# A recurrence beside a feed-forward block: loads of a later step moved behind a step's output matmuls, and a sigmoid moved into the step's outputs

## The chip, the cores and the metric

The kernel runs on one core of one Trainium2 chip. The time is the device time of one execution in microseconds (us). The core's engines work side by side, each through its own list of instructions in order: TensorE (PE in the profile; its weight loads are PEld), VectorE (DVE), ScalarE (ACT), GpSimd (POOL) and SyncE (SP), which here only issues DMA transfers. An instruction that must wait for another engine holds up all that stands behind it on its own engine; this holds for the transfers on SP's queue as well.

## The reference

Three stages follow one another. The first is a recurrence with a matrix state (an mLSTM) over 4 batches, 8 heads, 768 tokens, 40 numbers per head:

```python
for t in range(S):
    m_new = np.maximum(f_gate[:, :, t] + m, i_gate[:, :, t])
    f_stab = np.exp(f_gate[:, :, t] + m - m_new)
    i_stab = np.exp(i_gate[:, :, t] - m_new)
    C = f_stab * C + i_stab * np.einsum('bhd,bhe->bhde', vt, kt)
    n = f_stab * n + i_stab * kt
    y[:, :, t] = sigmoid(o_gate[:, :, t]) * (C @ q) / np.maximum(np.abs(n @ q), 1.0)
```

Its output, 3072 tokens of 320 numbers, goes through a gated block, `(sigmoid(x @ w_gate) * (x @ w_val)) @ w_out` with 1536 hidden numbers, and that through a second, `(h * relu6(h + 3) / 6) @ w_out` with 2048.

## The kernel before, in words

**The recurrence by steps.** The 768 tokens are cut into 6 chunks of 128. Within a chunk the recurrence is written as matrix products; between chunks the state `cst` goes on. One step is one chunk and one batch, named (c,b); there are 24. A step needs three loaded tiles: `qk` (queries and keys, L209), `vko` (values, keys by token, output gate, L212) and `dec`, the rows of decay factors, broadcast to all partitions (L220). Each of the three has two slots, so the tile of step b+2 lies where that of step b was, and its load waits until the last reader of step b is done: for `qk` the output matmuls (L442), for `dec` the matmuls of L453, for `vko` the gated output `yo` (L502), which VectorE makes.

**A step has three pieces.** `att0`: the scores (L360), the values with the input gate (`vi`, L351), two scans that make the decays (L386), two weightings of the scores with them (L401), and in the kernel before also the output gate's sigmoid (L407). `att1`: the matmuls of the outputs (L442, L453) and of the state (L468), the denominators (L485 to L494), `y` and `yo` (L351, L502), the state update (L523). `att2`: a transposition on TensorE (L534), split into a rounded and a remaining part (ScalarE L539, VectorE L540). The scores' PSUM banks are emptied by the weightings, and there are two such banks, which the scores, the outputs and the transposition share. So a transposition must wait for a weighting.

**The feed-forward block runs beside it.** `m1_h` makes 128 hidden numbers for 512 tokens: eight matmuls into one PSUM bank (L552 to L559), eight into another; ScalarE makes the sigmoid (`g`, L578), VectorE the product (L579), which empties the second bank, and both split it (`gh` L565, `gl` L566). `m1_out` multiplies with the output weights (L594, L604), one or two such steps later. The pool `mm` of PSUM has three banks; two are `m1_h`'s, and the state matmuls take one as well. Between two steps of the block, at most one or two pieces of the recurrence are put in, by a list of numbers (`quota`).

**The weights of the second block are prepared meanwhile.** Raw weights are fetched (`raw`, L92), made to float (L116, L119) and stored (`w_dram`, L619). From the fourth chunk on every second step of the block calls `combine_w2`: it loads one transfer into `wa` (L651) and four small ones into its second half (L656), makes sums and differences on VectorE (L663), splits them (ScalarE `ws` L667, VectorE L668 and L673) and stores them (`ws_dram`, L677). The last part, L668 and L673, is called the ws block below.

**What sets the order.** The program is traced in Python in the order of these calls, and a scheduler then places each instruction on its engine's list. In the main loop, the loads of the step after the next are traced behind piece 2 (L881 to L883):

```python
if cp > 0 and piece == 2 and nxt[0] < NC:
    att_load(*nxt)
    dec_load(*nxt)
```

Of the kernel before, what the change touches and what calls it, by code (L numbers as in the profile page):

```python
# [20 lines left out]
NC = S // L  # L21
# [11 lines left out]
def mlstm_then_two_gated_ffn(  # L33
# [159 lines left out]
    def slot_f32(n, p=P):  # L193

        return wpool.tile([P, 1280], F32, tag="w", name="early", bufs=18)[:p, :n]

    def att_tiles(c, b):
        if c == 0 and b > 1:
            t = slot_f32(2 * NP * L).rearrange("p (a n l) -> p a n l", a=2, l=L)
            v = slot_f32(3 * DM).rearrange("p (a n) -> p a n", a=3)  # L200
            d = slot_f32(H * L).rearrange("p (h l) -> p h l", l=L)
        else:
            t = ap.tile([P, 2, NP, L], F32, tag="qk", name="qk")
            v = ap.tile([P, 3, DM], F32, tag="vko", name="vko")
            d = ap.tile([P, H, L], F32, tag="dec", name="dec")
        at[c, b] = {"qk": t, "vko": v, "dec": d}

    def qk_load(c, b):
        nc.sync.dma_start(out=at[c, b]["qk"], in_=qkT[c, b])  # L209

    def vko_load(c, b):
        nc.sync.dma_start(out=at[c, b]["vko"], in_=vko[c, b])  # L212

    def att_load(c, b):
        att_tiles(c, b)
        qk_load(c, b)
        vko_load(c, b)

    def dec_load(c, b):
        nc.sync.dma_start(  # L220
            out=at[c, b]["dec"].rearrange("p h l -> p (h l)"),
            in_=fz_dram[c, b * H : (b + 1) * H, :]
            .rearrange("h l -> (h l)")
            .rearrange("(o n) -> o n", o=1)
            .to_broadcast([P, H * L]),
        )
# [28 lines left out]
    last_exp = []  # L255
# [98 lines left out]
    def scores(c, b, ps):  # L354
        a = at[c, b]
        qk = a["qk"]
        a["s"] = [ps(), ps()]
        for h in range(H):
            p0 = 64 * (h % 2)
            nc.tensor.matmul(  # L360
                out=a["s"][h % 2][:, (h // 2) * L : (h // 2 + 1) * L],
                lhsT=qk[p0 : p0 + D, 1, h // 2, :],
                rhs=qk[p0 : p0 + D, 0, h // 2, :],
                start=h < 2,
                stop=h >= H - 2,
                skip_group_check=True,
            )
# [37 lines left out]
    def out_gate(c, b):  # L405
        o = at[c, b]["vko"][:, 2, :]
        nc.scalar.activation(out=o, in_=o, func=AF.Sigmoid)  # L407

    def att0(c, b, ps):
        scores(c, b, ps)  # L410
        if c == 1:
            values(c, b, True)
        value_ones(c, b)
        for n in range(2):
            decays(c, b, n)
        if c != 1:
            values(c, b, False)
        if c < NC - 1:
            values_end(c, b, c == 0)
        for n in range(2):  # L420
            weigh(c, b, n)

        with tc.issue_after(last_exp[-1]):
            out_gate(c, b)

    def att1(c, b, ps):

        outputs(c, b, ps)
        y = denominators(c, b)
        gated(c, b, y, c == 1 and b < 2)  # L430
        state(c, b)

    def outputs(c, b, ps):
        a = at[c, b]
        dec, vi = a["dec"], a["vi"]

        halves = [slice(t, t + 32) for t in range(0, L, 32)]
        if c > 0:
            o_ps = a["o_ps"] = ps()
            for n in range(NP):  # L440
                for tt in halves:
                    nc.tensor.matmul(  # L442
                        out=o_ps[tt, n * 2 * D1 : (n + 1) * 2 * D1],
                        lhsT=a["qk"][:, 0, n, tt],
                        rhs=cst[:, b, n, :],
                        start=n == 0,
                        stop=n == NP - 1,
                        skip_group_check=True,
                    )
        i_ps = a["i_ps"] = ps()  # L450
        for h in range(H):
            for tt in halves:
                nc.tensor.matmul(  # L453
                    out=i_ps[tt, h * D1 : (h + 1) * D1],
                    lhsT=dec[:, h, tt],
                    rhs=vi[:, h, :],
                    start=h == 0,
                    stop=h == H - 1,
                    skip_group_check=True,
                )  # L460
        if c < NC - 1:
            k_on = a["vko"].rearrange("p a n -> p (a n)")[:, DM:]
            c_ps = c_banks[c, b] = ps() if ps is any_ps else ps_mm()
            for h in range(H):
                p0 = 64 * (h % 2)

                for d in (0, 32):
                    nc.tensor.matmul(  # L468
                        out=c_ps[p0 + d : p0 + d + 32, (h // 2) * D1 : (h // 2 + 1) * D1],
                        lhsT=k_on[:, h * D + d : h * D + d + 32],  # L470
                        rhs=a["vd"][:, h, :],
                        start=h < 2,
                        stop=h >= H - 2,
                        skip_group_check=True,
                    )

    def denominators(c, b):
        a = at[c, b]
        i_v = a["i_ps"][:, : H * D1].rearrange("p (h d) -> p h d", d=D1)
        y = i_v  # L480
        den = a["den"] = ap.tile([P, H, 1], F32, tag="den", name="den")
        if c > 0:
            y = ap.tile([P, H, D1], F32, tag="y", name="y")
            o_v = a["o_ps"][:, : H * D1].rearrange("p (h d) -> p h d", d=D1)
            nc.vector.tensor_tensor(  # L485
                out=y, in0=o_v, in1=gT[:, c, b].to_broadcast([P, H, D1]), op=ALU.mult
            )
            nc.vector.tensor_tensor(out=y, in0=y, in1=i_v, op=ALU.add)
        nq = y[:, :, D:D1]
        nc.vector.tensor_scalar(  # L490
            out=den, in0=nq, scalar1=-1.0, scalar2=1.0, op0=ALU.mult, op1=ALU.max
        )
        nc.vector.tensor_tensor(out=den, in0=den, in1=nq, op=ALU.max)
        nc.vector.reciprocal(out=den, in_=den)  # L494
        return y
# [77 lines left out]
    def m1_h(c, f, ts):  # L573
        n = ts.stop - ts.start
        banks = [ps_mm()[:, :n], ps_mm()[:, :n]]
        h_pair(slots["in", f], (1, c), banks, ts)
        g = gpool.tile([P, T], F32, tag="g", name="g")[:, :n]
        gate = nc.scalar.activation(out=g, in_=banks[0], func=AF.Sigmoid).ins  # L578
        nc.vector.tensor_tensor(out=g, in0=g, in1=banks[1], op=ALU.mult)  # L579
        gs[c, f, ts.start] = split_g(g)  # L580
        return gate
# [284 lines left out]
    for i, (c, f, ts) in enumerate(steps):  # L866
        if i == halves[0] - 1:
            for b in range(2):
                att_load(1, b)
                dec_load(1, b)  # L870
        for _ in range(quota[i]):
            if pieces:
                cp, b, piece = pieces.pop(0)
                if cp > 0 and b == 0 and piece == 0:
                    x_tiles((1, cp))
                with ExitStack() as queued:
                    for ins in opened if cp == 0 else ():
                        queued.enter_context(tc.issue_after(ins))
                    (att0, att1, att2)[piece](cp, b, ps_att)
                nxt = divmod(cp * B + b + 2, B)  # L880
                if cp > 0 and piece == 2 and nxt[0] < NC:  # L881
                    att_load(*nxt)
                    dec_load(*nxt)  # L883
        gate = m1_h(c, f, ts)
        outputs_but(2 if i < n_two else 1)
        before.append((c, f, ts))
        if c == 0:
            work(1 if i < 2 * halves[0] else 2, n_w1)
        elif c < NC - 1:

            with tc.issue_after(gate):
                work(c > 1 and f % 2 == 0, n_jobs)
                if c > 2 and f % 2 and combined < F2 // 2:
                    combine_w2(combined)
                    combined += 1
        elif f == 0:
            assert not jobs and not pieces and combined == F2 // 2
            early_sb.close()
            late = ctx.enter_context(tc.tile_pool(name="late", bufs=1, reuse_waits="tile"))
            x_loads = x_load(0)  # L900
            load_group(0)
        else:
            if f > 1 and f - 2 < F2 // 2:
                load_out2(f - 2)
            if f in (2, 5):
                x_combine(x_loads, f > 2)
# [180 lines left out]
```

## Time and profile before

| what | value |
|---|---|
| median of 3 runs | 862.91 us (861.52 to 864.82) |
| profiled execution | 860.47 us, span 858.6 us |
| mean granted clock | 0.997 |
| TensorE busy | 829.1 us, 97% of the span |
| weight loads of TensorE | 710.1 us, 83% |
| VectorE busy | 603.7 us, 70% |
| ScalarE busy | 413.2 us, 48% |
| the recurrence runs until about | 450 us |

The span is the time from the first to the last instruction in the profile. The granted clock is 1.00 where TensorE runs at 2.4 GHz and 0.50 where it runs at 1.2 GHz. In the rows below, a name such as L534 is a line of the kernel, `out<-in` are the tiles, and in brackets stands how long the engine had been idle and which instruction ended that. "SPq" is SP's queue, and a row of it is the issue of a transfer, not its time in flight.

### The profile page before, as it was taken

The numbers are of one execution on the slowest core, as the hardware profiler recorded it, in microseconds if no ns is written. First come the engines' busy times: TensorE is split into PE (matmuls) and PEld (weight loads), VectorE is DVE, ScalarE is ACT, GpSimd is POOL, SyncE is SP. The second block draws the span as 40 slices with busy tenths as digits, with TensorE's granted clock in tenths as the row PEclk, the third lists the DMA queues.
The fourth block names the chain that finished last, engine by engine and source line by source line (L and its number), as shares of the span: only waits on it lengthen the run. The fifth ranks groups of instructions, "written<-read, shape, count | busy, mean of one in ns | idle before, by whom it ended". The sixth has DMA issues, their size and how long they took to land.

```text
span 858.6 us, 17204 instructions
## 1 busy us (share of the span) xinstructions
PE 829.1 (97%) x7109; PEld 710.1 (83%) x7109; DVE 603.7 (70%) x1086; ACT 413.2 (48%) x821; POOL 2.5 (0%) x8
## 2 busy tenths in 40 slices
PE   6599899999999999998999999999999999999998
PEld 6489689888788787786888888888998889988898
DVE  7899975775576678988956734656766668665653
ACT  3687733322333343444425524656546555555542
POOL 1000000000000000000000000000000000000000
PEclk9999999999999999999999999999999999999999
DMA  9635733322555368887623503434404454033300
GB/s 345 234 126 198 260 98 111 126 94 73 173 171 165 124 241 265 274 268 254 208 99 116 156 1 110 177 138 177 144 32 142 159 199 144 32 129 134 124 31 32
DMA packets 41534, 130.65 MB, mean 152 GB/s; under 512 B 4592, under 2 KB 16048, under 8 KB 38384
## 3 DMA queue, kind: packets, MB, share of 16 engines
q1 hardware_dynamic: 41408, 129.45, 43.9%
q8 instruction: 56, 0.92, 0.4%
q14 instruction: 22, 0.18, 0.1%
q10 hardware_dynamic: 48, 0.10, 0.0%
HBM read 104.53 MB, written 25.00 MB: 151 GB/s over the span
## 4 chain that ended last, share of the span: by engine, by line
PE 79%; DVE 13%; DMA 4%; issue 2%; ACT 1%; SPq 0%; DVEq 0%; ACTq 0%
PE acc L594 9%; PE mm L920 9%; PE mm L558 6%; PE mm L556 6%; PE mm L557 6%; PE att L920 4%; PE acc L920 4%; PE mm L552 4%; PE acc L604 3%; PE mm L559 3%; PE mm L959 2%; PE mm L957 2%; PE acc L957 2%; PE mm L958 2%; PE acc L959 2%
## 5 line engine op out<-in xcount | busy, mean ns | idle before, releaser
L565 ACT CAST gh<-g 128x512 fp32r<-128x512 f32 (+1 forms) x130 | 76.4, 588 | 132.2 <-DVE g L579 110.4
L556 PE MATMUL mm<-x,w 128*128 128x512 f32 (+1 forms) x328 | 121.0, 369 | 0.0
L557 PE MATMUL mm<-x,w 128*128 128x512 f32 (+1 forms) x328 | 120.8, 368 | 0.0
L558 PE MATMUL mm<-x,w 128*128 128x512 f32 (+1 forms) x328 | 120.4, 367 | 0.0
L566 DVE TENSOR_TENSOR gl<-g,gh 128x512 fp32r<-128x512 f32 (+1 forms) x130 | 84.1, 647 | 51.2 <-ACT gh L565 50.8
L594 PE MATMUL acc<-gh,w 128*128 128x512 f32 (+1 forms) x328 | 104.4, 364 | 0.1
L920 PE MATMUL mm<-X,wg 128*128 128x512 f32 x336 | 84.3, 391 | 0.0
L579 DVE TENSOR_TENSOR g<-g,mm 128x512 f32<-128x512 f32 (+1 forms) x82 | 50.4, 615 | 34.6 <-PE mm L559 34.2
L920 PEld LDWEIGHTS mm<-X,wg 128*128 128x128 f32 x336 | 61.9, 188 | 12.6 <-DVE g L936 0.3
L557 PEld LDWEIGHTS mm<-x,w 128*128 128x128 f32 x328 | 62.8, 191 | 10.7
L558 PEld LDWEIGHTS mm<-x,w 128*128 128x128 f32 x328 | 62.6, 191 | 10.6
L556 PEld LDWEIGHTS mm<-x,w 128*128 128x128 f32 x328 | 62.8, 191 | 8.4
L594 PEld LDWEIGHTS acc<-gh,w 128*128 128x128 f32 x328 | 60.6, 189 | 10.7 <-ACT x L610 0.9
L552 PE MATMUL mm<-x,w 128*128 128x512 f32 (+1 forms) x164 | 66.8, 408 | 2.5 <-DVE cst L523 1.6
L578 ACT ACTIVATE g<-mm 128x512 f32<-128x512 f32 (+1 forms) x82 | 44.5, 543 | 44.0 <-PE mm L559 41.8
L386 DVE TENSOR_TENSOR_SCAN dec<-dec,ident 128x512 f32<-128x512 f32 x40 | 48.0, 1215 | 21.3 <-DMA dec<-fz_dram 21.3
L559 PE MATMUL mm<-x,w 128*128 128x512 f32 (+1 forms) x164 | 59.9, 365 | 0.0
L594 PE MATMUL acc<-gl,w 128*128 128x512 f32 (+1 forms) x164 | 59.8, 365 | 0.0
L935 ACT ACTIVATE gb<-c,half 128x512 f32<-128x512 f32 x48 | 34.6, 724 | 44.0 <-DVE c L931 43.7
L566 DVE TENSOR_TENSOR gl<-gb,gh 128x512 fp32r<-128x512 f32 x48 | 32.4, 690 | 24.2 <-ACT gh L565 24.1
L565 ACT CAST gh<-gb 128x512 fp32r<-128x512 f32 x48 | 29.5, 620 | 36.5 <-PE att L958 35.1
L920 PE MATMUL att<-X,wg 128*128 128x512 f32 x168 | 46.3, 395 | 0.0
(188 smaller groups left out, 1737.9 us busy)
## 6 DMA issues: line engine op xcount, KB each, us to landing
wg<-ws_dram SPq DMA_DIRECT2D x24, 1344.0 KB, 5.7
raw<-in_w SPq DMA_DIRECT2D x20, 640.0 KB, 4.3
qk<-in_qkT SPq DMA_DIRECT2D x22, 512.0 KB, 5.0
vko<-in_vko SPq DMA_DIRECT2D x22, 480.0 KB, 4.4
dec<-fz_dram SPq DMA_DIRECT2D x20, 512.0 KB, 5.8
raw<-in_wo SPq DMA_DIRECT2D x14, 640.0 KB, 4.5
ws_dram<-ws SPq DMA_DIRECT2D x8, 768.0 KB, 3.6
w_dram<-bits SPq DMA_DIRECT2D x16, 320.0 KB, 2.4
```

The source lines that it names most:

```text
L386: nc.vector.tensor_tensor_scan(out=x, data0=a["factors"][n] if "factors" in a else x, data1=ident4.rearrange("p h l -> p (h l)"), initial= ...
L552: nc.tensor.matmul(out=banks[j], lhsT=tail, rhs=xl[:, 2, :], start=True, stop=False)
L556: nc.tensor.matmul(out=banks[j], lhsT=hi, rhs=xh[:, k, :], start=False, stop=False)
L557: nc.tensor.matmul(out=banks[j], lhsT=hi, rhs=xl[:, k, :], start=False, stop=False)
L558: nc.tensor.matmul(out=banks[j], lhsT=lo, rhs=xh[:, k, :], start=False, stop=False)
L559: nc.tensor.matmul(out=banks[j], lhsT=tail, rhs=xh[:, 2, :], start=False, stop=True)
L565: nc.scalar.copy(out=gh, in_=g)
L566: nc.vector.tensor_tensor(out=gl, in0=g, in1=gh.bitcast(F32), op=ALU.subtract)
L578: gate = nc.scalar.activation(out=g, in_=banks[0], func=AF.Sigmoid).ins
L579: nc.vector.tensor_tensor(out=g, in0=g, in1=banks[1], op=ALU.mult)
L594: nc.tensor.matmul(out=a[m], lhsT=lhsT, rhs=rhs, start=st and lhsT is hi and rhs is gh, stop=en and lhsT is lo, skip_group_check=True,)
L920: nc.tensor.matmul(out=ps, lhsT=w[:, s, a, :], rhs=x[:, b, :], start=first and i == 0, stop=i == 3, skip_group_check=True,)
```

## The change

Two edits. The output gate's sigmoid is no longer traced at the end of `att0`, but in `att1`, behind the step's matmuls and ahead of the denominators. And the loads of the step after the next are traced behind piece 1 (`att1`), not behind piece 2 (`att2` of the same step, which comes later), in another order: the decay rows, then `qk`, then `vko`.

```diff
--- before.py
+++ after.py
@@ -420,12 +420,11 @@
         for n in range(2):
             weigh(c, b, n)
 
+    def att1(c, b, ps):
+
+        outputs(c, b, ps)
         with tc.issue_after(last_exp[-1]):
             out_gate(c, b)
-
-    def att1(c, b, ps):
-
-        outputs(c, b, ps)
         y = denominators(c, b)
         gated(c, b, y, c == 1 and b < 2)
         state(c, b)
@@ -878,9 +877,11 @@
                         queued.enter_context(tc.issue_after(ins))
                     (att0, att1, att2)[piece](cp, b, ps_att)
                 nxt = divmod(cp * B + b + 2, B)
-                if cp > 0 and piece == 2 and nxt[0] < NC:
-                    att_load(*nxt)
+                if cp > 0 and piece == 1 and nxt[0] < NC:
+                    att_tiles(*nxt)
                     dec_load(*nxt)
+                    qk_load(*nxt)
+                    vko_load(*nxt)
         gate = m1_h(c, f, ts)
         outputs_but(2 if i < n_two else 1)
         before.append((c, f, ts))
```

No instruction is added or taken away. Below, line numbers between 426 and 880 are one lower in the changed kernel (L501 is L502 before). On SP's queue the loads of most steps stand where they stood. Changed are: (1,2) and (1,3), decay rows ahead of one fetch of raw weights; (2,1), decay rows ahead of `vko`; and the steps from (4,3) on, in which the decay rows come first.

On SP, around the load of step (5,0), before (`dec<-fz_dram` is its decay rows, `vko<-in_vko` its values):

```order
L209 DMA qk<-in_qkT 128x1024
L220 DMA dec<-fz_dram 128x1024
L677 DMA ws_dram<-ws 128x1536
L677 DMA ws_dram<-ws 128x1152
L651 DMA wa<-w_dram 128x4x128
L656 DMA wa<-w_dram 32x4x128 x4
L212 DMA vko<-in_vko 128x960
L619 DMA w_dram<-bits 128x640
L92 DMA raw<-in_wo 128x640
```

and after the change:

```order
L220 DMA dec<-fz_dram 128x1024
L209 DMA qk<-in_qkT 128x1024
L676 DMA ws_dram<-ws 128x1536
L676 DMA ws_dram<-ws 128x1152
L650 DMA wa<-w_dram 128x4x128
L212 DMA vko<-in_vko 128x960
L655 DMA wa<-w_dram 32x4x128 x4
L618 DMA w_dram<-bits 128x640
L92 DMA raw<-in_wo 128x640
```

The decay rows go ahead of `qk`, and `vko` goes from behind the four small loads of `wa` to ahead of them. Step (5,1) has a like change a little later: all three loads stand ahead of the store of `w_dram`.

On VectorE, around the outputs of step (4,2), before (`dec_4604` is the decay tile of (5,0), `yo_4473` the output of (4,2), `dec_4353` the decay tile of (4,3)):

```order
L490 TENSOR_SCALAR den_4465<-y_4466 128x8
L493 TENSOR_TENSOR den_4465<-den_4465,y_4466 128x8
L579 TENSOR_TENSOR g_4498<-g_4498,mm_4481 128x512
L494 RECIPROCAL den_4465<-den_4465 128x8
L386 SCALAR_TENSOR_TENSOR dec_4604<-dec_4604,ident4_81 128x512
L351 TENSOR_TENSOR y_4466<-y_4466,den_4465 128x8x40
L566 TENSOR_TENSOR gl_4502<-g_4498,gh_4501 128x512
L502 TENSOR_TENSOR yo_4473<-y_4466,vko_4087 128x320
L386 SCALAR_TENSOR_TENSOR dec_4604<-dec_4604,ident4_81 128x512
L401 TENSOR_TENSOR dec_4353<-att_4535,dec_4353 128x4x128
```

and after (`dec_4482` is the decay tile of (5,0)):

```order
L489 TENSOR_SCALAR den_4465<-y_4466 128x8
L386 SCALAR_TENSOR_TENSOR dec_4482<-dec_4482,ident4_81 128x512
L492 TENSOR_TENSOR den_4465<-den_4465,y_4466 128x8
L578 TENSOR_TENSOR g_4504<-g_4504,mm_4487 128x512
L493 RECIPROCAL den_4465<-den_4465 128x8
L386 SCALAR_TENSOR_TENSOR dec_4482<-dec_4482,ident4_81 128x512
L351 TENSOR_TENSOR y_4466<-y_4466,den_4465 128x8x40
L565 TENSOR_TENSOR gl_4508<-g_4504,gh_4507 128x512
L501 TENSOR_TENSOR yo_4473<-y_4466,vko_3954 128x320
L401 TENSOR_TENSOR dec_4231<-att_4541,dec_4231 128x4x128
```

Both scans of (5,0) now stand ahead of `y` and `yo`; before, the second stood behind them. A few rows later `vi` of (5,0), which reads `vko`, and `gl` and `x` now stand ahead of `wa`; before, `wa` stood ahead of `x` and `vi`.

On VectorE, some 30 rows later, around the weighting of (5,0), before (`dec_4794` is the decay tile of (5,1), `dec_4604` that of (5,0)):

```order
L540 TENSOR_TENSOR x_3809<-att_4786,x_3809 128x3x128
L663 TENSOR_TENSOR wa_4641<-wa_4641 128x256 x4
L668 TENSOR_TENSOR ws_4651<-wa_4641,ws_4651 128x4x128
L673 TENSOR_TENSOR ws_4651<-wa_4641,ws_4651 32x4x128 x2
L668 TENSOR_TENSOR ws_4657<-wa_4641,ws_4657 128x3x128
L673 TENSOR_TENSOR ws_4657<-wa_4641,ws_4657 32x3x128 x2
L579 TENSOR_TENSOR g_4816<-g_4816,mm_4799 128x512
L401 TENSOR_TENSOR dec_4604<-att_4854,dec_4604 128x4x128
L401 TENSOR_TENSOR dec_4604<-att_4855,dec_4604 128x4x128
L566 TENSOR_TENSOR gl_4820<-g_4816,gh_4819 128x512
L386 SCALAR_TENSOR_TENSOR dec_4794<-dec_4794,ident4_81 128x512 x2
```

and after (`dec_4747` is the decay tile of (5,1), `dec_4482` that of (5,0)):

```order
L539 TENSOR_TENSOR x_3809<-att_4792,x_3809 128x3x128
L662 TENSOR_TENSOR wa_4640<-wa_4640 128x256 x4
L386 SCALAR_TENSOR_TENSOR dec_4747<-dec_4747,ident4_81 128x512 x2
L667 TENSOR_TENSOR ws_4650<-wa_4640,ws_4650 128x4x128
L672 TENSOR_TENSOR ws_4650<-wa_4640,ws_4650 32x4x128 x2
L667 TENSOR_TENSOR ws_4656<-wa_4640,ws_4656 128x3x128
L672 TENSOR_TENSOR ws_4656<-wa_4640,ws_4656 32x3x128 x2
L578 TENSOR_TENSOR g_4816<-g_4816,mm_4799 128x512
L401 TENSOR_TENSOR dec_4482<-att_4854,dec_4482 128x4x128
L401 TENSOR_TENSOR dec_4482<-att_4855,dec_4482 128x4x128
L565 TENSOR_TENSOR gl_4820<-g_4816,gh_4819 128x512
```

The two scans of (5,1) go from behind the weighting of (5,0) to ahead of the ws block.

On ScalarE the sigmoid of the output gate (L407) goes to places behind the step's `vi` copy (L380); those of the steps from (5,0) on still stand about where they stood.

## Rows read from the trace of the kernel before

**Rows 1.** Waits of TensorE, 40 to 450 us: total us, times, longest.

```profile
PE att L534 <- DVE dec L401: 4.9, 4, 2.2
PE mm L552 <- DVE cst L523: 1.6, 1, 1.6
PE mm L552 <- ACT g L578: 0.9, 2, 0.5
```

**Rows 2.** Timeline of TensorE: start and duration in us, wait before in brackets.

```profile
100.61 0.50 PE L552 MATMUL mm<-x,w 128*128 128x512 f32 x1 [1.62 <-DVE cst L523]
...
396.04 0.55 PE L534 MATMUL att<-ident,yo 128*128 128x128 f32 x3 [2.23 <-DVE dec L401]
```

**Rows 3.** Windows: PE, PEld, DVE, ACT, POOL busy, granted clock, DMA, GB/s.

```profile
396.60:400.00 3.40, 3.26 (x8) 2.05 (x8) 3.40 (x5) 1.76 (x5) 0.00 (x0) 0.50 0.80 266
```

**Rows 4.** Waits of SP's queue, 40 to 450 us.

```profile
SPq L209 <- PE att L442: 88.2, 13, 16.3
...
SPq L212 <- DVE yo L502: 30.7, 15, 3.0
```

**Rows 5.** Waits of VectorE and ScalarE, 40 to 450 us.

```profile
DVE dec L386 <- DMA dec<-fz_dram: 21.3, 10, 4.6
...
ACT vko L407 <- DMA vko<-in_vko: 20.6, 8, 4.3
```

**Rows 6.** Timeline of VectorE, 349 to 370 us.

```profile
352.35 0.48 DVE L502 TENSOR_TENSOR yo<-y,vko 128x320 f32<-128x320 f32 x1
352.75 1.22 DVE L386 TENSOR_TENSOR_SCAN dec<-dec,ident 128x512 f32<-128x512 f32 x1
353.88 1.26 DVE L401 TENSOR_TENSOR dec<-att,dec 128x512 f32<-128x512 f32 x2
...
356.92 0.42 DVE L663 TENSOR_TENSOR wa<-wa 128x256 f32<-128x256 f32 x1
...
360.22 0.69 DVE L668 TENSOR_TENSOR ws<-wa,ws 128x512 fp32r<-128x512 f32 x1
...
364.06 0.69 DVE L579 TENSOR_TENSOR g<-g,mm 128x512 f32<-128x512 f32 x1
```

**Rows 7.** Timeline of SP's queue, 342 to 373 us.

```profile
349.98 2.61 SPq L656 DMA_DIRECT2D wa<-w_dram  x4
352.90 0.35 SPq L212 DMA_DIRECT2D vko<-in_vko  x1
```

**Rows 8.** DMA issues: count, KB each, median us to landing.

```profile
vko<-in_vko SPq DMA_DIRECT2D x22, 480.0 KB, 4.4
...
xr<-x_dram SPq DMA_DIRECT2D x48, 64.0 KB, 2.1
...
wa<-w_dram SPq DMA_DIRECT2D x32, 64.0 KB, 4.2
```

**Rows 9.** Timeline of SP's queue, 310 to 330 us.

```profile
319.95 3.41 SPq L656 DMA_DIRECT2D wa<-w_dram  x4
```

**Rows 10.** Timeline of VectorE, 318 to 336 us.

```profile
326.91 1.55 DVE L663 TENSOR_TENSOR wa<-wa 128x256 f32<-128x256 f32 x4 [1.88 <-DMA wa<-w_dram]
```

**Rows 11.** Timeline of VectorE, 370 to 397 us.

```profile
372.21 1.55 DVE L663 TENSOR_TENSOR wa<-wa 128x256 f32<-128x256 f32 x4
374.54 0.69 DVE L668 TENSOR_TENSOR ws<-wa,ws 128x512 fp32r<-128x512 f32 x1 [0.78 <-ACT ws L667]
...
378.98 1.28 DVE L401 TENSOR_TENSOR dec<-att,dec 128x512 f32<-128x512 f32 x2
...
380.78 2.33 DVE L386 TENSOR_TENSOR_SCAN dec<-dec,ident 128x512 f32<-128x512 f32 x2
...
395.30 1.28 DVE L401 TENSOR_TENSOR dec<-att,dec 128x512 f32<-128x512 f32 x2
```

**Rows 12.** Timeline of TensorE, 363 to 382 us.

```profile
365.38 0.40 PE L552 MATMUL mm<-x,w 128*128 128x512 f32 x1
...
381.74 0.78 PE L442 MATMUL att<-cst,qk 128*32 128x82 f32 x32
```

## The prediction

> **What bounds the kernel now.** I read the table first: TensorE is busy 97% of the span, so only the remaining stalls of TensorE, and the clock, can change the time. The waits of TensorE between 40 and 450 us, where the recurrence runs, say where those are [rows 1]: four waits of the transposes (L534) for the weighting of the decay tiles (L401), 4.9 us together, one wait of a gate matmul (L552) for the state update (L523), 1.6 us, and two for the sigmoid of ScalarE, 0.9 us. That is 7.4 us in all; no rearrangement of the recurrence gives back more than that, plus what the clock lost behind them. The longest of the four [rows 2] stands at 396.04, 2.23 us, and right behind it the granted clock is 0.50, that is 1.2 GHz, over the 3.4 us of [rows 3]: half of that, 1.7 us, is lost. So 3.9 us hang on one place, and the reader should see that L401 is VectorE's.
>
> Second, what the change aims at. On the queue of SP the load of qk waits 88.2 us in 13 places for output matmuls (L442), that of vko 30.7 us for yo [rows 4]. Those waits are the buffers' own: the tiles have two slots, so a load cannot go before its slot is empty, and the change does not alter that. What follows from late loads is seen in [rows 5]: VectorE waited 21.3 us for decay rows, ScalarE 20.6 us for vko. Neither is TensorE.
>
> **The change part by part.**
>
> *The sigmoid of the output gate (L407)* goes from the step before to the step's own outputs. Same instructions. The 20.6 us of ScalarE's idle time mostly go, but TensorE waits 0.9 us for ScalarE in the whole stretch [rows 1], so I price this at zero; the cover is ScalarE's idle half.
>
> *The order of the loads.* Most of the steps keep their place on SP (the section on the change says which do not), since their slots come free when they did. The three stalls of the transposes before 390 us are not behind a moved load: for those I take zero.
>
> *The place around 98 us.* VectorE has one scan less ahead of the state update and one weight conversion more. The two short stalls and the one of 1.62 us [rows 1, 2] become one; I take +0.1 us, ends −0.9 (the two short ones go) and +1.1 (one scan's length, as in [rows 6]).
>
> *The place from 350 us, which decides.* In the order on SP, vko of step (5,0) moves from behind the four tail loads of wa to ahead of them; on VectorE the second scan moves from behind yo to ahead of it.
> 1. A scan takes 1.13 us from its start to the next start (352.75 to 353.88) [rows 6]. Now it stands ahead of yo, which ended at 352.83: it ends at about 353.96.
> 2. vko needs yo's end, and SP is in order, so the tails wait behind it. They had been issued from 349.98 on, 2.61 us for the four, with vko behind them at 352.90 [rows 7]. Now vko is issued at 353.96, the tails from 354.4 to 357.0, the last one at about 356.4.
> 3. They land 4.2 us later by the median of the wa tails [rows 8]: 360.6. A second measure: at 326.91 VectorE began the same work, after waiting for it, 3.55 us behind the end (319.95 + 3.41 = 323.36) of the four issues [rows 9, 10], which gives 357.0 + 3.55 = 360.55. Beside it, vko lands 4.4 us after its issue [rows 8], at 358.4, and the chain that now stands ahead of wa on VectorE (vi, gl, x; with ScalarE's gate and gh between) ends near 360.5 as well.
> 4. So wa (L663), at 356.92 before [rows 6], starts at 360.6. From wa to the next ws is 2.33 us (372.21 to 374.54) [rows 11]: 362.9; from ws to the next g (L579) it is 3.84 us (360.22 to 364.06) [rows 6]: 366.75, which is 2.7 us late.
> 5. TensorE reached the gate matmul that needs the bank which this g empties at 365.38 [rows 12]; the g ended at 364.75, so 0.63 us were free. The new stall is 2.7 − 0.63, about **2.0 us**.
> 6. Both scans of (5,1) now stand ahead of the next ws block; they stood at 380.78, 2.33 us for both [rows 11]. They use 0.78 us of idle time there and push the block by 1.55 us: the weighting of (5,0), which began at 378.98 and took 1.28 us, ends near 384.5, against outputs that start at 381.74 + 2.0 [rows 11, 12]: 0 to 0.8 us more.
> 7. Behind that, VectorE has 2.33 us less to do up to the weighting of (5,1), at 395.30 [rows 11], and loses 0.7 us where gl has nothing ahead of it while gh is made: late by 2.7 + 1.55 − 2.33 + 0.7 = 2.6 us. TensorE is 2.0 to 2.8 us late itself, so the stall of 2.23 us stays at its size.
>
> From there all is 2.0 to 2.8 us late; I take **+2.4**. If the tails land at once the ends are 0, if they land as late as 6 us, +4. The clock I leave where it was: once at half.
>
> Sum: 0 + 0 + 0.1 + 2.4 = **+2.5 us** on the profiled execution's 860.47, so 863.0. The median of the runs shown is 2.44 us higher, at 862.91, so the forecast is **865.4 us**, 0.3% more. A measurement tells about 0.5%, 4.3 us here, from no change: this is inside.
>
> **The rivals.**
>
> *Faster: the scans come out of the way.* Steps 6 and 7 without steps 2 to 5. If vko leaves on time (yo is not held up, or the tails land in the idle time), the scans of (5,1) fill the 0.78 us and VectorE reaches the weighting of (5,1) earlier; the stall of 2.23 us, the half clock of 1.7 and the 0.9 at 90 to 97 us can go: −4.8 us, 858.1. For it: the order does put the scans early, and they no longer wait for decay rows. Against it: the tails stand behind a wait for yo, which is late by the same scan. The point from which it decides: wa at 357.5 or before.
>
> *Slower: the clock follows the new stall.* The 2.23 us stall was followed by half clock [rows 2, 3]; the one of 1.62 us [rows 2] was not. The new one of 2.0 us lies between, and a stall of 2.6 us in one piece near 98 us would be beyond both. Each costs 1.7 us: 2.5 + 1.7 to 2.5 + 3.4 us, so 867.1 to 868.8.
>
> *No change.* The issues moved are hidden and wa is not late: 862.9 to 863.5. Most steps' loads do keep their place, so that the change hardly does what it says is part of this case. A transfer of 64 KB can be quick: xr's land in 2.1 us, as against 4.2 for wa's tails [rows 8]; at 2.1 the tails are there at 358.5. Then vi, waiting for vko until 358.4, would still hold wa near 360.5; only if vko is as quick too does the delay end. The Trainium skill, in "DMA: Bandwidth & Descriptors" (Anatomy of one DMA), states a fit, for GpSimd's path, of 2.0 us and the bytes over 436 GB/s; an estimate by that page is 2.15 us for a tail and 3.1 us for vko, by which wa would start near 358.8, g would be 0.9 us late, the stall 0.3 us and the sum about +0.4. The trace differs for this kernel's wa and vko (4.2 and 4.4 us), and the measurement decides.
>
> **How the numbers follow.** The forecast 0.33, most of it within 0.5% (0.05 beyond, where wa's tails are late by more); slower by the clock 0.32 (0.25 beyond 0.5%); faster 0.25 (0.20 beyond); no change 0.10. That makes faster 0.20, same 0.50 (0.28 + 0.07 + 0.05 + 0.10), slower 0.30. The range reaches down to the faster rival and above the slower one: 858.0 to 869.5; the forecast's own is 863.0 to 867.0.
>
> **What would show it.** Right: vko of (5,0) issued near 354 with the four tails behind it; wa waiting for a DMA until 360 to 361; a new stall of some 2 us of L552 behind L579 near 365; the stall of L534 near 396 still above 1.9 us. Wrong: wa before 358, no stall at 365, or the weighting of (5,1) done before TensorE's transposes come; then the faster rival holds. A clock below 1.00 between 366 and 371, or near 102, is the slower one.

## The result, and the profile after

The changed kernel takes **869.48 us** (median of 4 runs, 868.99 to 870.39), the kernel before 862.21 us (median of 4 runs). The ratio is 1.008, with a 95% interval of 1.0056 to 1.0104: 0.8% slower, by more than a measurement of this kernel can mistake. The forecast was 865.4 us; the result lies 0.02 us below the upper end of the range, and nearest to the rival in which the clock makes it slower (867.1 to 868.8 us). All medians here are of undisturbed executions; one, of `x1` below, took 2,833 us and is left out.

The profiled execution after took 868.99 us, its span is 867.1 us, 8.5 us more than before. TensorE is busy for 830.8 us against 829.1: it does the same work, so the time went into waits and into work at half clock. The waits of TensorE, of the kernel after, 40 to 450 us, with columns as in [rows 1]:

```profile
PE att L533 <- DVE dec L401: 7.2, 4, 2.8
PE mm L551 <- DVE cst L522: 2.9, 1, 2.9
PE mm L551 <- DVE g L578: 1.3, 1, 1.3
PE att L360 <- DVE x L539: 1.3, 1, 1.3
PE acc L593 <- ACT x L609: 0.5, 1, 0.5
PE mm L551 <- ACT g L577: 0.3, 1, 0.3
```

They sum to 13.5 us, against 7.4 us in [rows 1]. Three rows are new: L551 behind the product `g` (L578), the scores (L360) behind `x` (L539), and the output matmuls (L593) behind ScalarE's `x` (L609). The one behind the state update has gone from 1.6 to 2.9 us, and the transpositions' from 4.9 to 7.2.

Of the waits that the change aims at [rows 5], ScalarE's for `vko` have gone from 20.6 to 3.8 us; VectorE's for the decay rows, 21.3 us before, have not become less:

```profile
ACT vko L407 <- DMA vko<-in_vko: 3.8, 2, 2.6
DVE dec L386 <- DMA dec<-fz_dram: 23.1, 11, 4.1
```

Where the two executions part is seen when the same matmul is looked up in both. Each bank of `m1_h` begins with one L552 (L551 after), 164 in the whole kernel; the k-th of them began at (us):

| k-th L552 | before | after | after minus before | what lies in between |
|---|---|---|---|---|
| 26 | 100.61 | 99.71 | -0.90 | |
| 27 | 105.56 | 106.26 | +0.70 | half clock |
| 35 | 129.73 | 130.28 | +0.55 | |
| 45 | 149.29 | 151.64 | +2.35 | the scores wait for `x` |
| 47 | 153.98 | 157.79 | +3.81 | half clock |
| 75 | 234.72 | 238.97 | +4.25 | |
| 105 | 335.60 | 340.99 | +5.39 | a longer wait of L533 |
| 114 | 365.38 | 372.24 | +6.86 | L551 waits for `g` |
| 125 | 407.29 | 415.47 | +8.18 | longer waits of L533 and of the output matmuls near 404 |

The 0.90 us of the first row are no gain of the change: in the six kernels below that are the kernel before up to here (x3, x4, y1, y2, y3, z1), the 26th began between 99.27 and 99.97 us.

The half clock shows in the windows of the kernel after (PE, PEld, DVE, ACT and POOL busy, granted clock, DMA, GB/s):

```profile
20.00:40.00 20.00, 9.62 (x184) 7.54 (x188) 17.57 (x39) 10.43 (x31) 0.00 (x0) 0.55 0.66 228
...
102.00:106.00 4.00, 4.00 (x25) 3.02 (x25) 3.67 (x8) 3.04 (x11) 0.00 (x0) 0.78 0.55 178
...
152.00:156.00 4.00, 4.00 (x24) 4.00 (x23) 1.80 (x4) 0.38 (x1) 0.00 (x0) 0.63 0.00 0
370.00:376.00 6.00, 4.66 (x20) 3.39 (x20) 5.22 (x13) 2.92 (x7) 0.00 (x0) 1.00 0.87 300
404.00:408.00 4.00, 4.00 (x13) 3.20 (x13) 4.00 (x6) 1.39 (x3) 0.00 (x0) 0.57 0.65 190
```

It stands behind the wait of 2.93 us near 99 us, behind that of 1.34 us near 150 us, and near 404 us (before, near 397 us); behind the new wait near 372 us the clock stays at 1.00. In the window 20 to 40 us it was at half as well (0.55, before 1.00), and there nothing was lost: the 11th L552, at 62.89 us, began at the same time in both. (The clock was at half there in x4 and y1 too, whose 11th began at 62.23 and 62.10 us; in y2, y3, x3 and z1, where it was not, at 61.57 to 62.27 us.)

**The place near 150 us**, which the prediction priced at zero. Timeline of VectorE, kernel after:

```profile
147.38 1.22 DVE L386 TENSOR_TENSOR_SCAN dec<-dec,ident 128x512 f32<-128x512 f32 x1 [2.19 <-DMA dec<-fz_dram]
...
148.84 1.22 DVE L386 TENSOR_TENSOR_SCAN dec<-dec,ident 128x512 f32<-128x512 f32 x1
149.97 0.53 DVE L539 TENSOR_TENSOR x<-att,x 128x384 fp32r<-128x384 f32 x1
```

and of TensorE:

```profile
148.73 0.48 PE L360 MATMUL att<-qk 40*128 40x128 f32 x2
150.56 1.16 PE L360 MATMUL att<-qk 40*128 40x128 f32 x14 [1.34 <-DVE x L539]
```

The same place in the kernel before, VectorE:

```profile
147.59 0.56 DVE L540 TENSOR_TENSOR x<-att,x 128x384 fp32r<-128x384 f32 x1
148.07 2.33 DVE L386 TENSOR_TENSOR_SCAN dec<-dec,ident 128x512 f32<-128x512 f32 x2
```

Before, `x` came first and both scans behind it. After, the decay rows of (2,1) are issued ahead of `vko`, the scheduler puts the scans ahead of `x`, and VectorE waits 2.19 us for the decay rows with `x` behind it. The scores need the PSUM bank that `x` empties: two of sixteen matmuls go, then TensorE stalls.

**The place from 350 us**, kernel after: SP's queue,

```profile
359.26 0.33 SPq L212 DMA_DIRECT2D vko<-in_vko  x1
359.65 1.85 SPq L655 DMA_DIRECT2D wa<-w_dram  x4
```

VectorE,

```profile
363.19 0.49 DVE L351 TENSOR_TENSOR vi<-vko,iT 128x320 f32<-128x320 f32 x1 [0.56 <-DMA vko<-in_vko]
364.26 0.69 DVE L565 TENSOR_TENSOR gl<-g,gh 128x512 fp32r<-128x512 f32 x1 [0.58 <-ACT gh L564]
...
365.34 1.54 DVE L662 TENSOR_TENSOR wa<-wa 128x256 f32<-128x256 f32 x4
...
371.50 0.69 DVE L578 TENSOR_TENSOR g<-g,mm 128x512 f32<-128x512 f32 x1
```

ScalarE,

```profile
363.25 0.47 ACT L407 ACTIVATE vko<-vko 128x320 f32<-128x320 f32 x1 [2.60 <-DMA vko<-in_vko]
363.62 0.60 ACT L564 CAST gh<-g 128x512 fp32r<-128x512 f32 x1
```

and TensorE:

```profile
372.24 0.50 PE L551 MATMUL mm<-x,w 128*128 128x512 f32 x1 [1.34 <-DVE g L578]
```

As forecast, `vko` goes only when `yo` is done (at 359.26 us, 5.3 us behind the forecast's 353.96; 5.4 us had been lost by the 105th L552), the four tails stand behind it, `wa` comes late, `g` comes late, and L551 waits. What releases `wa` (L662, no idle time before it) is not the tails but the chain from `vko`: `vi` waits for it, the sigmoid waits for it, `gh` stands behind the sigmoid on ScalarE and `gl` behind `gh`. The margin is small: the last tail, issued at 361.07 us, landed 4.1 us later, some 0.2 us ahead of `wa`.

### The profile page after: what moved, and what is told of

It reads as the page before. It is cut to its first block, busy times and chain, and to the rows that moved or that the text cites. A ratio compares the mean times of both kernels' runs of the same rounds, so it can differ in the third digit from the quotient of the medians.

```text
span 867.1 us, 17214 instructions
## 1 busy us (share of the span) xinstructions
PE 830.8 (96%) x7109; PEld 711.9 (82%) x7109; DVE 604.0 (70%) x1086; ACT 414.2 (48%) x821; POOL 2.5 (0%) x8
## 4 chain that ended last, share of the span: by engine, by line
PE 75%; DVE 16%; DMA 3%; issue 3%; ACT 1%; SPq 1%; DVEq 0%; ACTq 0%
PE acc L593 9%; PE mm L921 8%; PE mm L556 6%; PE mm L557 6%; PE mm L555 6%; PE att L921 4%; PE acc L921 4%; PE mm L551 3%; PE acc L603 3%; PE mm L558 3%; DVE dec L386 2%; PE mm L958 2%; PE mm L960 2%; PE mm L959 2%; PE acc L958 2%
## 5 line engine op out<-in xcount | busy, mean ns | idle before, releaser
L593 PE MATMUL acc<-gh,w 128*128 128x512 f32 (+1 forms) x328 | 104.6, 365 | 0.5 <-ACT x L609 0.5
L578 DVE TENSOR_TENSOR g<-g,mm 128x512 f32<-128x512 f32 (+1 forms) x82 | 50.4, 615 | 41.8 <-PE mm L558 41.6
L551 PE MATMUL mm<-x,w 128*128 128x512 f32 (+1 forms) x164 | 67.2, 410 | 4.6 <-DVE cst L522 2.9
L593 PEld LDWEIGHTS acc<-gh,w 128*128 128x128 f32 x328 | 60.8, 190 | 11.1 <-ACT x L609 1.0
L593 PE MATMUL acc<-gl,w 128*128 128x512 f32 (+1 forms) x164 | 59.8, 365 | 0.0
```

The source lines that it names most:

```text
L551: nc.tensor.matmul(out=banks[j], lhsT=tail, rhs=xl[:, 2, :], start=True, stop=False)
L593: nc.tensor.matmul(out=a[m], lhsT=lhsT, rhs=rhs, start=st and lhsT is hi and rhs is gh, stop=en and lhsT is lo, skip_group_check=True,)
```

## The experiments

All but x1b were timed against the kernel before on the same chip; its medians were 861.0 to 861.7 us. Differences are of medians, ratios have their 95% interval. The lines of `x1` and `z4` are one lower than those of the kernel before between 426 and 880, those of `z1` some higher.

**x1: the sigmoid's move alone.** The first edit of the change, without the second.

> The sigmoid's move alone; loads as before. Theory (three places: the sigmoid reorders VectorE before 110 us, the loads cause the rest): the stall near 99 us is 2.5 to 3 us in one piece and half clock follows, all else as before, so 0 to +1.5 us against the kernel before. Rival A (the sigmoid's move holds ScalarE at 360 us and causes the stall behind L578 too): +3 us or more.

862.91 against 861.69 us, ratio 1.0015 (1.0005 to 1.0026): +1.2 us. The profile is of a further execution of the same kernel:

> The sigmoid's move alone once more, for its profile: one stall of 2.5 to 3 us behind the state update near 99 us in place of the three of 0.5, 0.4 and 1.6 us, with 1.2 GHz behind it; stalls near 161, 335 and 394 us at the lines where they were, each within 1 us of its size; no stall near 149 or 365 us.

Timeline of TensorE of that profile (863.68 us):

```profile
95.43 0.50 PE L551 MATMUL mm<-x,w 128*128 128x512 f32 x1 [0.39 <-ACT g L577]
...
100.48 0.50 PE L551 MATMUL mm<-x,w 128*128 128x512 f32 x1 [2.94 <-DVE cst L522]
```

The three waits have become 0.39 and 2.94 us, 3.33 us in place of 2.52, at a clock of 1.00 behind them in this execution, where half clock was expected. There is no stall near 149 or 365 us; the one near 335 us is 2.09 us, 1.1 us more than before, of which more below. So the sigmoid's move is not free: +0.1 was forecast for this place, and the whole edit costs 1.2 us. Rival A falls.

**x2: the loads' move alone.** The second edit without the first.

> The loads' move alone; sigmoid as before. Theory: stalls near 99 us as before (0.5, 0.4 and 1.6 us), but the stall of the scores near 149 us of 1.3 us with half clock behind it, and the one near 365 us of 1 to 2 us, so +5 to +7 us. Rival A: 0 to +3 us, since the sigmoid's half is missing. Rival B (the transfers themselves are slower in this order): the waits for decay rows near 159 and 172 us grow by 0.6 us each although their place is unchanged.

869.14 against 861.69 us, ratio 1.008 (1.0064 to 1.0096): +7.5 us, somewhat more than expected; the interval (5.5 to 8.3 us) reaches into what was. Both new stalls are there without the sigmoid's move: that of the scores is 1.26 us, and half clock follows it, as it follows the other. TensorE, and the windows behind the two stalls,

```profile
374.40 0.50 PE L552 MATMUL mm<-x,w 128*128 128x512 f32 x1 [2.39 <-DVE g L579]
```

```profile
151.00:154.00 3.00, 3.00 (x16) 2.78 (x15) 1.68 (x4) 0.52 (x2) 0.00 (x0) 0.50 0.02 5
376.00:379.00 3.00, 3.00 (x9) 2.35 (x8) 2.10 (x8) 2.17 (x5) 0.00 (x0) 0.50 0.87 215
```

and VectorE of this run:

```profile
367.48 1.55 DVE L663 TENSOR_TENSOR wa<-wa 128x256 f32<-128x256 f32 x4 [0.69 <-DMA wa<-w_dram]
```

Here VectorE did wait for the tails, 0.69 us more than for the chain from `vko`: the two come within a microsecond of each other, as step 3 had it. Of rival B the trace shows nothing firm: TensorE's waits near 166 and 178 us were 1.32 and 0.27 us, against 1.58 and 0.16 us before.

**x3: the load of (2,1) alone.**

```diff
-                if cp > 0 and piece == 2 and nxt[0] < NC:
-                    att_load(*nxt)
-                    dec_load(*nxt)
+                if cp > 0 and piece == (1 if nxt == (2, 1) else 2) and nxt[0] < NC:
+                    att_tiles(*nxt)
+                    if nxt == (2, 1):
+                        dec_load(*nxt)
+                    qk_load(*nxt)
+                    vko_load(*nxt)
+                    if not nxt == (2, 1):
+                        dec_load(*nxt)
```

> The load of step (2,1) alone as changed (decay rows first, behind piece 1), all else as before. Theory: the stall of 1.3 us near 149 us with 1.2 GHz behind it, +2 to +3.5 us, nothing at 365. Rival (half clock there is chance): the stall alone, +1.3 us or less.

863.19 against 861.69 us, ratio 1.0021 (1.0006 to 1.0035): +1.5 us. TensorE:

```profile
149.05 1.16 PE L360 MATMUL att<-qk 40*128 40x128 f32 x14 [1.49 <-DVE x L540]
```

The stall is there, and the clock stays at 1.00 behind it in this execution; the kernel after and x2 had half clock here. The time lies between the rival (+1.3 us or less) and the theory (+2 or more), and its interval, 0.5 to 3.0 us, reaches into both.

**z1: the same, with `x` first.** As x3, and the scans of (2,1) are told to be placed behind `x` of (1,3) (two lines that note each `x` in `x_done`, and the edit of x3, are left out here):

```diff
-        for n in range(2):
-            decays(c, b, n)
+        with ExitStack() as late:
+            if (c, b) == (2, 1):
+                late.enter_context(tc.issue_after(x_done[1, 3]))
+            for n in range(2):
+                decays(c, b, n)
```

> As the run with the load of step (2,1) alone (decay rows still first and early), but the two scans of (2,1) are placed behind x of (1,3) on VectorE. Theory (x waits behind scans that wait for decay rows): the stall of the scores near 149 us is gone, 0 to +0.3 us against the kernel before. Rival (the early transfer of decay rows itself is the cost): +1 to +2 us as in that run.

860.96 against 861.02 us, ratio 0.9995 (0.9986 to 1.0004). SP's order is that of x3; on VectorE only the places of `x`, the scans and `vi` differ. Its VectorE:

```profile
145.19 0.56 DVE L544 TENSOR_TENSOR x<-att,x 128x384 fp32r<-128x384 f32 x1
145.73 2.34 DVE L387 TENSOR_TENSOR_SCAN dec<-dec,ident 128x512 f32<-128x512 f32 x2
```

TensorE does not stall there. So the cost of x3 is the order on VectorE, not the earlier transfer.

**x4: the load of (5,0) alone.** The edit of x3 with (5, 0) in place of (2, 1).

> The load of step (5,0) alone as changed. Theory: vko waits for the later yo, the four tails of wa wait behind it, wa starts 2 to 3 us late, TensorE stalls 1 to 2 us near 365 us behind L579: +1.5 to +3 us. Rival C (the scans of (5,1), which stay behind the weighting here, were the cost): 0 to +1 us.

865.92 against 861.69 us, ratio 1.0042 (1.003 to 1.0054): +4.2 us, more than was expected. TensorE:

```profile
368.24 0.50 PE L552 MATMUL mm<-x,w 128*128 128x512 f32 x1 [1.50 <-DVE g L579]
```

The stall itself is 1.5 us. Much of the rest lies near 404 us, where the scheduler has changed ScalarE's list as well. Before, the copy `x` (L610), which empties the output matmuls' bank, stood ahead of `gh`:

```profile
398.55 1.07 ACT L610 COPY x<-acc 128x512 f32<-128x512 f32 x2 [1.42 <-DMA ws_dram<-ws]
399.84 0.62 ACT L565 CAST gh<-g 128x512 fp32r<-128x512 f32 x1 [0.22 <-DVE g L579]
```

In x4 it stands behind `gh`, which waits for VectorE's product, and TensorE waits for it 2.11 us, where it had waited 0.1 us before:

```profile
403.59 0.62 ACT L565 CAST gh<-g 128x512 fp32r<-128x512 f32 x1 [2.71 <-DVE g L579]
404.12 1.07 ACT L610 COPY x<-acc 128x512 f32<-128x512 f32 x2
404.75 0.55 PE L594 MATMUL acc<-gh,w 128*128 128x512 f32 x1 [2.11 <-ACT x L610]
```

The order is the same in x2, y2 and the kernel after. One wait alone would say little, since it varies: the waits of TensorE at this place, for L401 and then for ScalarE's or VectorE's `x`, are 4.9 us together in x4, and 2.4 to 3.3 us in the five profiles with the old order there (before, y1, x3, z1, x1b). How much of the 4.2 us is due to this order was not tested by itself. Rival C falls: the scans of (5,1) stayed where they were.

**y1 and y2: the two halves of that edit.** In y1 the decay rows and `qk` of (5,0) go behind piece 1, `vko` stays behind piece 2; in y2 all three go behind piece 1, in the old order.

```diff
 # y1
-                if cp > 0 and piece == 2 and nxt[0] < NC:
-                    att_load(*nxt)
-                    dec_load(*nxt)
+                if cp > 0 and piece == (1 if nxt == (5, 0) else 2) and nxt[0] < NC:
+                    att_tiles(*nxt)
+                    if nxt == (5, 0):
+                        dec_load(*nxt)
+                    qk_load(*nxt)
+                    if not nxt == (5, 0):
+                        vko_load(*nxt)
+                        dec_load(*nxt)
+                if piece == 2 and nxt == (5, 0):
+                    vko_load(*nxt)
 # y2
-                if cp > 0 and piece == 2 and nxt[0] < NC:
+                if cp > 0 and piece == (1 if nxt == (5, 0) else 2) and nxt[0] < NC:
                     att_load(*nxt)
                     dec_load(*nxt)
```

> Of step (5,0) decay rows and qk go behind piece 1, vko stays behind piece 2: on SP vko stays behind the four tails of wa, on VectorE the second scan still goes ahead of yo. Theory (vko ahead of the tails is the cost): 0 to +0.5 us, no stall behind L579 near 365 us. Rival (the scan ahead of yo is the cost): +1.5 us or more with that stall.

> The load of step (5,0) behind piece 1 in the old order (qk, vko, decay rows): vko goes ahead of the tails of wa, the second scan stays behind yo. Theory: wa is late, by some 1 us less than with the scan ahead of yo as well; a stall of 0.3 to 1.5 us behind L579 near 365 us, +1 to +3 us in all. Rival (the scan ahead of yo is the cost): 0 to +0.5 us.

y1: 861.71 against 861.29 us, ratio 1.0005 (0.9997 to 1.0014), +0.4 us. y2: 864.65 us, ratio 1.004 (1.0026 to 1.0055), +3.4 us, a little above what was expected. SP's queue in y1,

```profile
349.80 2.99 SPq L656 DMA_DIRECT2D wa<-w_dram  x4
354.99 0.35 SPq L212 DMA_DIRECT2D vko<-in_vko  x1
```

and in y2:

```profile
354.43 0.33 SPq L212 DMA_DIRECT2D vko<-in_vko  x1
354.81 0.43 SPq L651 DMA_DIRECT2D wa<-w_dram  x1
355.29 1.92 SPq L656 DMA_DIRECT2D wa<-w_dram  x4
```

TensorE in y2:

```profile
368.38 0.50 PE L552 MATMUL mm<-x,w 128*128 128x512 f32 x1 [1.33 <-DVE g L579]
```

In y1 `vko` goes late too, since the scan stands ahead of `yo`, but the tails have gone 5 us earlier than in y2, VectorE keeps `wa` ahead of `vi`, and there is no stall. In y2 no scan stands ahead of `yo`, and yet the stall is there: all five transfers of `wa` stand behind one that waits for `yo`. The price lies in the place of `vko` on SP's queue, and in the order of `vi` and the sigmoid that the scheduler makes of it; no run tells these two apart.

Near 400 us the three engines have the same order in y2 as in x4, and the clock falls at another point. From 400 to 404 us it was 0.57 in y2 and 1.00 in x4. So y2 does the matmuls ahead of the wait for `x` more slowly and then waits 0.53 us, where x4 waits 2.11 us; the output matmuls start at 404.87 and 404.75 us. Half clock ahead of that wait cost next to nothing; in x4 it came behind it (0.63 in 404 to 408 us).

**y3: the loads of (5,1) to (5,3) alone.** The edit of x3 with the condition `nxt >= (5, 1)`.

> Only the loads of steps (5,1) to (5,3) as changed: on VectorE both scans of (5,1) go ahead of the ws block that precedes the weighting of (5,0). Theory: the scans use idle time of VectorE there, the stall of 2.2 us near 394 us shrinks by 0.5 to 1.5 us, no other place changes: -2 to 0 us. Rival (the scans push the ws block and with it the weighting of (5,0) past TensorE's need): 0 to +2 us, with a new stall near 382 us.

861.57 against 861.29 us, ratio 1.0001 (0.9991 to 1.0012). TensorE:

```profile
396.28 0.55 PE L534 MATMUL att<-ident,yo 128*128 128x128 f32 x3 [1.16 <-DVE dec L401]
...
401.43 0.50 PE L604 MATMUL acc<-gh,w 128*128 128x512 f32 x1 [1.64 <-DVE x L615]
```

The stall of 2.23 us [rows 2] is 1.16 us here, with the scans now ahead of the ws block, and five microseconds later the output matmuls wait 1.64 us for `x` (L615), which empties their banks. But x1b and z1, whose lists there are those of the kernel before, have such a pair too: 1.47 and 1.81 us, 1.43 and 1.84 us. So this profile does not show that the scans made the stall shorter. What y3 shows is the time: the mechanism of the faster rival, on its own, is worth nothing (-0.8 to +1.0 us). Nor is there a new stall near 382 us.

**z4: the whole change without (2,1) and (5,0).** Both edits, the loads of these two steps as before.

> The whole change, but the loads of steps (2,1) and (5,0) as before. Theory (these two steps carry the loads' part): what the sigmoid's move costs alone is left, +0.5 to +2 us; no stall near 149 or behind L579 near 365 us. Rival (the rest of the loads has a share of its own): +3 us or more.

863.55 against 861.02 us, ratio 1.0032 (1.002 to 1.0043): +2.5 us, between theory and rival, and more than x1's 1.2 us. There is no stall near 149 or 365 us. That near 99 us is 2.94 us, and in this execution half clock follows it, as in the kernel after (windows of z4):

```profile
102.00:106.00 4.00, 4.00 (x22) 2.94 (x23) 3.72 (x7) 2.86 (x10) 0.00 (x0) 0.72 0.49 170
```

The interval (1.7 to 3.7 us) overlaps that of x1 (0.4 to 2.2 us), so a share of the remaining loads of 1 us or so is neither shown nor excluded.

**z5 and v6: two attempts at a faster kernel.** z5 is the kernel before with the four small loads of `wa` issued by GpSimd:

```diff
-            nc.sync.dma_start(out=a[r : r + 32, 0:4, 1, :], in_=tail)
+            nc.gpsimd.dma_start(out=a[r : r + 32, 0:4, 1, :], in_=tail)
```

> The kernel before with the four small loads of wa issued by GpSimd, which has nothing else to do, so that they stand in no other transfer's way on SP's queue. If VectorE's wait for wa before the stall near 335 us is set by SP's issue of these four (some 3 us), wa starts 1 to 2 us earlier there and the stall of L534 with the half clock behind it shrinks: -1 to -4 us. Rival (these transfers land later when GpSimd issues them, or the scheduler's other order makes new waits): 0 to +5 us.

881.24 against 861.02 us, ratio 1.0231 (1.0216 to 1.0246): +20.2 us, far beyond both expectations. The transfers land later (median us in the last column),

```profile
wa<-w_dram SPq DMA_DIRECT2D x8, 256.0 KB, 4.3
wa<-w_dram POOLq DMA_DIRECT2D x32, 64.0 KB, 5.1
```

5.1 against 4.2 us [rows 8], and with the scheduler's new order TensorE waits 2.6 to 4.4 us at four places; what each of the two costs was not separated. v6 takes `combine_w2` out of two steps of the block:

```diff
-                if c > 2 and f % 2 and combined < F2 // 2:
+                if c > 2 and f % 2 and (c, f) not in ((3, 3), (3, 11)) and combined < F2 // 2:
```

> The kernel before (loads and sigmoid untouched), but combine_w2 is left out behind two steps of the block (the second and the sixth odd one of the fourth chunk) and so done two steps of its own later: VectorE then weighs (4,1) and (5,1) ahead of a ws block. Theory (the stalls of L534 near 335 and 394 us are weighting behind a ws block): both shrink below 0.7 us and no half clock follows there, -2 to -6 us, if the later blocks near 410 to 450 us make no new stall. Rival (what is gained is given back at the next wait, as with the loads of (5,1)): -1 to +1 us.

863.13 against 861.25 us, ratio 1.0021 (1.0009 to 1.0033): +1.9 us, slower than either expectation. Both stalls are gone, near 335 and near 396 us, and one of L534 has come in their place, with half clock behind it (0.51 in 358 to 365 us):

```profile
358.97 0.90 PE L534 MATMUL att<-ident,yo 128*128 128x128 f32 x3 [3.30 <-DVE dec L401]
```

No version that was run beats the kernel before.

## Why the prediction was right in part, and where it failed

- **The sum of the parts.** The sigmoid cost +1.2 us (x1), the load of (2,1) +1.5 us (x3), that of (5,0) +4.2 us (x4): together +6.9 us, and the change measured +7.3 (869.48 against 862.21). Forecast were +0.1, 0 and +2.4. The sum fits only within its intervals (0.4 to 2.2, 0.5 to 3.0 and 2.6 to 4.7 us): another split, x1 and x2, gives +8.7.
- **That the time lies within the range was luck.** The forecast's own sum was +2.5 us, a third of what came. The upper end was set for a clock that falls behind two stalls; the time got there by a stall that was priced at zero, a sigmoid that was priced at almost zero, and a place that cost nearly twice its price.
- **"The order of the loads", a zero in the sum: this step failed, for (2,1).** The prediction looked there at the three stalls of the transpositions only ("for those I take zero"). The decay rows of (2,1) had changed place on SP, as the section on the change says; the order on VectorE behind them was not followed to the end. Scans that may go earlier take the place of `x`, and wait for a transfer with `x` behind them: a stall of 1.26 to 1.49 us in three profiles (after, x2, x3), +1.5 us in time (x3), nothing with `x` first (z1).
- **The place from 350 us, steps 1 to 5: right in the main mechanism, short in size.** `vko` was issued 5.3 us behind its forecast time, with 5.4 us lost by then (the 105th L552); `wa` at 365.34, forecast 360.6 and the drift make 366.0; the stall of L551 was 1.34 us, forecast 2.0. But step 1, the scan ahead of `yo`, is no cause by itself (y1 +0.4 us), and x4 lost 4.2 us where +2.4 was forecast: 1.5 in the stall, much of the rest at the waits behind it. In step 3, `wa` was to wait for the tails; after, the chain from `vko` held it, which step 3 put at the same time, and in x2 the tails did. Step 7 had the stall near 396 us keep its size; it was 2.82 us after and 2.76 in x4, and the wait for ScalarE's `x` a few us later, 2.11 us in x4, was not in the sum at all: the new order of `gh` and `x` on ScalarE had not been looked for.
- **The sigmoid "at zero", with 0.1 us for the place near 98 us: too little.** The one stall of 2.6 us was right in kind (2.93), but 0.33 us of the two waits for ScalarE stayed beside it, so that 2.52 us became 3.26 after and 3.33 in x1b. Half clock followed in two profiles (after and z4), not in x1b; what it adds to the 1.2 us was not measured. ScalarE's idle time did go, as was said; it bought nothing.
- **The stalls near 161, 175 and 335 us, "for those I take zero": right for the first and the last as far as is seen, misread in size.** That near 335 us was 2.06 us after and 0.97 us in the profile of before, whose TensorE shows

```profile
335.29 0.55 PE L534 MATMUL att<-ident,yo 128*128 128x128 f32 x3 [0.97 <-DVE dec L401]
```

  But it was 2.02, 2.14, 2.35 and 2.63 us in x4, y1, y2 and y3, in which no engine's list differs from the kernel before ahead of it. VectorE's wait for `wa` ahead of that stall, 1.88 us in [rows 10], was 2.50, 2.61, 2.81 and 3.07 us there. So 0.97 was the low end of a spread, and that 1.1 us between the two profiles is not the change's. The stall near 175 us was 0.71 to 0.98 us in the three profiles with the sigmoid moved (z4, after, x1b), and at most 0.34 us in the others but x3 (0.92). A part of the sigmoid's cost may lie there; that is not shown.
- **The slower rival came closest in time**, and half by its mechanism: half clock behind the stall near 99 us, none behind the one near 372 (in x2 it did follow there). Its point of decision (between 1.6 and 2.2 us) does not hold: half clock followed 1.34 us near 150 us, 1.26 us in x2, and not 2.94 us in x1b.
- **The faster rival fell in y3**: the scans of (5,1) went early as it has them, and the time stayed.
- The fit of the Trainium skill, "DMA: Bandwidth & Descriptors" (Anatomy of one DMA), stated for GpSimd's path, 2.0 us and the bytes over 436 GB/s, gave an estimate of 3.1 us for `vko`. Here VectorE had it at 363.19, 3.93 us behind its issue by SP: the measured time holds, and with it the delay. The start of `wa` at 358.8 that the prediction drew from this estimate leaves out the chain behind `vko`, 2.1 us by its own step 3, which would end at 359.2.

## What to carry to other kernels

A load that may go earlier does not go alone: here the scheduler put its consumers earlier as well, and what then stood behind them waited for the transfer. So follow the consumers of each moved load on their engines' lists, and who waits for what stands behind them, and look on an in-order queue for the transfers that come to stand behind one that waits. A stall that one edit cures is worth only what the next wait leaves of it (v6). And before a difference between two profiles is put down to a change, look how far profiles of kernels differ that are the same up to there.

## What the runs showed of the hardware

- Half clock is not a fixed price of a stall. Behind waits of one place it came in some executions and not in others: near 150 us with 1.34 us (after: 0.63 of full speed in 152 to 156 us) and with 1.26 us (x2: 0.50 in 151 to 154 us), not with 1.49 us (x3: 1.00); near 100 us with 2.93 us (after) and 2.94 us (z4), not with 2.94 us (x1b). Behind the new wait near 370 us it came with 2.39 us (x2: 0.50 in 376 to 379 us), not with 1.34 us (after: 1.00).
- Half clock cost nothing where TensorE waited anyway. In 23 to 41 us the clock was at half in the kernel after, and the 11th L552, at 62.89 us, came no later: TensorE stood 5.6 us of it in one wait for VectorE's L401, before as after. Near 400 us, y2 at half clock and x4 at full clock started the output matmuls 0.12 us apart.
- One and the same transfer, the tails of `wa`, in kernels that do not differ ahead of it, lets VectorE wait from 1.88 to 3.07 us, and L534 behind it from 0.97 to 2.63 us near 335 us. A price read from a single profile has that width.
